# Buffers of their own for the turned queries and rows of maxima of one chunk of a linear attention and gated feed-forward kernel

## Chip, cores and metric

The program runs on one core of a Trainium2 chip. The metric is the device time of one execution in microseconds (us). Runs of the kernel before the change are given as the median of three.

## What is computed

Linear attention over 8 sequences of 576 tokens with 8 heads of 64, then a gated feed-forward over all 4608 tokens:

```python
q_s = exp(q - max(q, axis=-1)); q_s = q_s / (sum(q_s, axis=-1) + 1e-9)   # over a head's 64 entries
k_s = exp(k - max(k, axis=2));  k_s = k_s / (sum(k_s, axis=2) + 1e-9)    # over the tokens
kv  = einsum('bhsd,bhse->bhde', k_s, v)
x   = einsum('bhsd,bhde->bhse', q_s, kv)          # laid out as 4608 tokens x 512
out = ((x @ w_a) * (x @ w_b)) @ w_out             # 512 -> 1536 -> 512, all float32
```

## The kernel before

**Tiling.** The tokens are cut into 9 chunks of 512 (`c` = 0 to 8). The heads go in 4 pairs (`g` = 0 to 3), each with 128 features on the 128 partitions. For a chunk, attention gives `xf` (features by tokens), and the feed-forward takes it as its right-hand operand. Chunk 0 is done while the weights are converted from 64-bit words; from chunk 1 on the main loop runs over `c`, and inside it over 6 blocks `i` of 256 hidden features.

**Feed-forward.** Each block does seven products in the manner of Strassen and Winograd (`product`, L449, into the PSUM tiles `kx`, `ky`, `ka`, `kp`). A product is 12 matmuls of 128x256: two gates, two halves of the contraction, and three terms of a float32 number split in a high and a low part. The weights of each product (`ws`, 512 KB, 8 buffers) come from DRAM every time (`get_w`, L165). VectorE (DVE) and ScalarE (ACT) join the products in `cc` (L698 to L727) and split the gated result in `gh` and `gl`; `project` (L470) multiplies by `w_out` into `po`.

**Attention of the next chunk.** While chunk `c` is in the feed-forward, the attention of chunk `c + 1` is put between its instructions. `attention_tasks` returns a list of steps, and `Spread` hands out one of them at each of three calls per block (`attend`). What a step gives to DVE is queued behind the DVE instruction passed to the call (`issue_after`); loads, ScalarE and TensorE work have no such tie. From chunk 2 on (`LATE` = 2) a query is read twice: in token order (`qt`), for the maxima and the sums (`q_stats`), and turned (`qtt`, features by tokens), for the product. `q_stats_out` turns the statistics of all four pairs on TensorE (`pst`) and writes them to DRAM (`dq`). From there every head's row of negative maxima and row of reciprocal sums is read back, copied to 64 partitions (`mr`). `q_exp` adds the maxima (L354), takes the exponential (L355) and splits the result in `qh` and `ql` (L79, L82); `x_product` multiplies (`px`, L381), and L562 multiplies by the reciprocal sums into `xf`. These are the steps b0 (loads), b1 (`q_exp`) and b2 (product), in a pipeline over `g`: b0 of one pair stands in the step of b1 of the pair before it.

**Buffers.** `qtt` shares the two buffers of tag `kt` with the keys of the batch that the same chunk needs. `mr` has two buffers, `qh` and `ql` one each. Tag `wy` (8 buffers of 128x512) holds weights while they are converted and the sums of weight blocks that chunk 1 needs, and lies idle after that.

**Order.** A scheduler sets the order of each engine's instructions at build time, with a timeline of its own; at run time every engine works through its list in that order. All loads and stores of data are issued by SyncE (SP), in one list. A load waits there until its buffer is free, and everything behind it waits too. The loads use eight completion semaphores in turn, so a load also waits until the one eight places before it has landed.

Of the kernel before, what the change touches and what calls it, by code (L numbers as in the profile page):

```python
# [7 lines left out]
F32 = mybir.dt.float32  # L8
F32R = mybir.dt.float32r
# [4 lines left out]
ALU = mybir.AluOpType  # L14
# [15 lines left out]
def linear_attention_then_gated_ffn(  # L30
# [18 lines left out]
    nc = tc.nc  # L49
    B, NP, P, J, _, D = k.shape  # L50
# [4 lines left out]
    T = 512  # L55
# [20 lines left out]
    def split(hi, lo, src, hi_engine="act"):  # L76

        if hi_engine == "act":
            nc.scalar.copy(out=hi, in_=src)  # L79
        else:  # L80
            nc.vector.tensor_copy(out=hi, in_=src)
        nc.vector.tensor_tensor(out=lo, in0=src, in1=hi.bitcast(F32), op=ALU.subtract)  # L82
# [151 lines left out]
    def kv_soft_t(kt, tags):  # L234

        kf = kt.rearrange("p j c -> p (j c)")
        mc = sb.tile([P, 1], F32, name="mc")
        nc.vector.tensor_reduce(out=mc, in_=kf, axis=AX.X, op=ALU.max, negate=True)
        nc.scalar.activation(out=kf, in_=kf, func=AF.Exp, bias=mc)
        pa = ps.tile([P, J - 1, P], F32, name="pka", tag=tags[0])  # L240
        pb = ps.tile([P, P], F32, name="pkb", tag=tags[1])
        for j in range(J):
            nc.tensor.transpose(pa[:, j] if j < J - 1 else pb, kt[:, j], ident)
        nc.scalar.copy(out=kt[:, 0:J - 1], in_=pa)
        nc.vector.tensor_copy(out=kt[:, J - 1], in_=pb)
        return kt.rearrange("p j (h d) -> p j h d", h=2)

    def kv_product(kt, vt, tag="at"):
        pk = ps.tile([P, 2, D + 1], F32, name="pk", tag=tag)
        for j in range(J):  # L250
            nc.tensor.matmul(  # L251
                pk, kt[:, j].rearrange("p h d -> p (h d)"), vt[:, j],
                start=(j == 0), stop=(j == J - 1),
            )
        den = sb.tile([P, 1], F32, name="den")
        nc.vector.tensor_scalar_add(den, pk[:, 0, D:D + 1], EPS)
        nc.vector.reciprocal(out=den, in_=den)
# [83 lines left out]
    def q_turned(c, g, dq):  # L341

        qt = sb.tile([P, T], F32, name="qtt", tag="kt")
        nc.sync.dma_start(out=qt, in_=qt_late[c - LATE, g])
        mr = sb.tile([P, 2, T], F32, name="mr", bufs=2)
        for h in range(2):
            nc.sync.dma_start(
                out=mr[h * D:(h + 1) * D].rearrange("d w t -> d (w t)"),
                in_=dq[g, h].unsqueeze(0).broadcast_to([D, 2 * T]),
            )  # L350
        return qt, mr

    def q_exp(qt, mr):
        nc.vector.tensor_tensor(out=qt, in0=qt, in1=mr[:, 0], op=ALU.add)  # L354
        nc.scalar.activation(out=qt, in_=qt, func=AF.Exp)  # L355
# [132 lines left out]
    xfs = {}  # L488

    def attention_tasks(c):  # L490

        xfs[c] = sb.tile([P, NP, T], F32, name="xf", bufs=1)
        steps = []
        for b in range(c * T // S, (c * T + T - 1) // S + 1):
            if b in batch_done:
                continue
            batch_done.add(b)
            for g in range(NP):
                box = {}
# [12 lines left out]
        def pipeline(steps):  # L512

            parts = max((len(p) for p in steps), default=0)
            return [
                [steps[i - j][j] for j in range(parts) if 0 <= i - j < len(steps)]
                for i in range(len(steps) + parts - 1)
            ]

        if c < LATE:  # L520
            for g in range(NP):
                box = {}

# [12 lines left out]
        stats, last = [], []  # L536
        every = {}
        for g in range(NP):
            box = {}

            def a0(g=g, box=box):
                if g == 0:
                    every["st"] = sb.tile([P, NP, 2, 2, TT], F32, name="st", bufs=1)
                box["q"] = q_load(c, g)

            def a1(g=g, box=box):
                q_stats(box["q"], every["st"][:, g])
                if g == NP - 1:
# [5 lines left out]
            def b0(g=g, box=box):  # L554
                box["q"] = q_turned(c, g, every["dq"])

            def b1(box=box):
                box["e"] = q_exp(*box["q"])

            def b2(g=g, box=box):  # L560
                px = x_product(c, g, box["e"])
                nc.vector.tensor_tensor(out=xfs[c][:, g], in0=px, in1=box["q"][1][:, 1], op=ALU.mult)  # L562

            last.append((b0, b1, b2))
# [46 lines left out]
    for g in range(NP):  # L611
        kt, vt, qt = first[g]
        odd = g % 2
        kt = kv_soft_t(kt, (("at", "k0"), ("k1", "k2"))[odd])
# [5 lines left out]
        qhl = q_transpose(qt, ("at", "k1")[odd])  # L620
        px = x_product(0, g, qhl, ("po2", "po3")[odd])
# [43 lines left out]
    last = None  # L665
    for c in range(1, NCH):
# [4 lines left out]
        for i in range(NI):  # L671
# [29 lines left out]
            last = nc.vector.tensor_tensor(out=u3, in0=ka, in1=u2, op=ALU.add)  # L701
# [13 lines left out]
            last = nc.vector.tensor_tensor(out=cc[:, 3, 0], in0=cc[:, 3, 0], in1=cc[:, 3, 1], op=ALU.mult)  # L715
# [11 lines left out]
            last = nc.vector.tensor_tensor(out=cc[:, 2, 0], in0=cc[:, 2, 0], in1=cc[:, 2, 1], op=ALU.mult)  # L727
# [55 lines left out]
```

## Time and profile before

| | |
|---|---|
| runs | 988.35, 990.72, 991.26 us (median 990.72) |
| profiled execution | 984.57 us, of which the span from first to last instruction is 982.6 |
| mean granted TensorE clock | 0.991 |
| TensorE matmuls (PE) | busy 948.5 us, 6171 of them |
| weight loads of TensorE (PEld) | busy 851.9 us |
| VectorE (DVE) | busy 629.2 us |
| ScalarE (ACT) | busy 391.4 us |
| GpSimd (POOL) | busy 112.8 us |
| data queue of SyncE | 282.57 MB, 82.3% of the 16 DMA engines' time |

The feed-forward of chunk 2 starts at about 269.5 us of the span, that of chunk 3 at 371.3, of chunk 4 at 475.4, of chunk 5 at 576.8, of chunk 6 at 678.6, of chunk 7 at 780.6, of chunk 8 at 878.9. In the period of chunk `c` stands the attention of chunk `c + 1`. How to read it: "idle before <-releaser" is time in which an engine waited, and what ended the wait; idle time of an engine that nobody waits for costs nothing. A row of waits gives total time, number and the longest.

### The profile page before, as it was taken

Reading aid. Unit: us, or ns where it says so; the run is one execution under the profiler, and the core shown is the slowest. Engines: PE = TensorE matmul, PEld = TensorE weight load, DVE = VectorE, ACT = ScalarE, POOL = GpSimd, SP = SyncE. Lnnn points to the kernel's source line nnn. Section 1 sums busy time; section 2 is a strip of 40 time slices with the busy share of each in tenths; the row PEclk is TensorE's granted clock in tenths of the full one; section 3 lists DMA queues with packets and bytes.
Section 4 is the critical chain, followed back from the end, with each engine's and each line's share of the span. In section 5 each row is a group of like instructions: output and inputs, shape, how many; then the busy total and the mean of one; then the engine's idle time right before and its main releaser. Section 6 shows DMA issues by size and latency. Waiting matters only on the chain.

```text
span 982.6 us, 16989 instructions
## 1 busy us (share of the span) xinstructions
PE 948.5 (97%) x6171; PEld 851.9 (87%) x6171; DVE 629.2 (64%) x1257; ACT 391.4 (40%) x1085; POOL 112.8 (11%) x96
## 2 busy tenths in 40 slices
PE   4889999999999999999999999999999999999998
PEld 3657666899999999989999999999999999899997
DVE  7797786887685656656576557655666546653433
ACT  8665675632273325322442235223532263221101
POOL 3245345441000000000000000000000000000000
PEclk9799999999999999999999999999999999999999
DMA  9699858999989968997799779977998689767761
GB/s 347 222 412 402 343 207 294 373 327 305 301 285 352 320 237 280 325 328 250 248 335 324 271 251 345 319 270 257 331 299 299 220 300 283 274 224 271 246 207 61
DMA packets 93682, 283.64 MB, mean 289 GB/s; under 512 B 10848, under 2 KB 11424, under 8 KB 93600
## 3 DMA queue, kind: packets, MB, share of 16 engines
q1 hardware_dynamic: 93600, 282.57, 82.3%
q8 instruction: 49, 0.80, 0.3%
q14 instruction: 33, 0.27, 0.1%
HBM read 241.40 MB, written 37.98 MB: 284 GB/s over the span
## 4 chain that ended last, share of the span: by engine, by line
PE 78%; DMA 8%; DVE 5%; issue 4%; POOL 2%; ACT 2%; SPq 0%; POOLq 0%; DVEq 0%; ACTq 0%
PE po L470 25%; PE kp L449 13%; PE kx L449 13%; PE ka L449 12%; PE ky L449 6%; PE pk L251 3%; PE px L381 2%; POOL wr L103 2%; DMA mr<-dq 2%; PE po L459 2%; PE pt L426 2%; DMA qtt<-in_q_late 1%; DMA wo_raw<-in_w_out 1%; DMA dw<-ws 1%; DVE ws L82 1%
## 5 line engine op out<-in xcount | busy, mean ns | idle before, releaser
L470 PE MATMUL po<-wo_w,gh 128*128 128x512 f32 x768 | 227.2, 394 | 0.0
L449 PE MATMUL kx<-xo,ws 128*128 128x256 f32 x1152 | 164.5, 284 | 0.0
L449 PE MATMUL ka<-xo,ws 128*128 128x256 f32 x1152 | 162.3, 284 | 0.2
L470 PEld LDWEIGHTS po<-wo_w,gh 128*128 128x128 f32 x768 | 138.9, 189 | 26.2 <-ACT gh L79 0.3
L449 PE MATMUL kp<-xo,ws 128*128 128x256 f32 x1152 | 158.3, 284 | 0.8 <-DVE cc L712 0.8
L449 PEld LDWEIGHTS ka<-xo,ws 128*128 128x128 f32 x1152 | 151.2, 191 | 4.0 <-ACT xo L79 0.3
L449 PEld LDWEIGHTS kx<-xo,ws 128*128 128x128 f32 x1152 | 151.6, 191 | 3.4 <-issue 0.5
L449 PEld LDWEIGHTS kp<-xo,ws 128*128 128x128 f32 x1152 | 148.2, 191 | 3.6 <-DVE cc L712 1.0
L470 PE MATMUL po<-wo_w,gl 128*128 128x512 f32 x384 | 137.7, 396 | 0.0
L79 ACT CAST gh<-cc 128x512 fp32r<-128x512 f32 x96 | 57.7, 620 | 148.5 <-DVE cc L723 145.1
L722 DVE TENSOR_TENSOR cc<-kp,u 128x512 f32<-128x512 f32 x48 | 33.0, 688 | 89.2 <-PE kp L449 89.0
L323 ACT ACTIVATE qt<-qt,st 128x64 f32<-128x64 f32 x224 | 75.0, 337 | 31.7 <-DVE st L320 27.8
L470 PEld LDWEIGHTS po<-wo_w,gl 128*128 128x128 f32 x384 | 71.2, 188 | 15.8 <-DVE gl L82 0.4
L449 PE MATMUL ky<-xo,ws 128*128 128x256 f32 x576 | 79.4, 287 | 2.5 <-ACT xo L79 2.1
L426 PE MATMUL pt<-xo,ws 128*128 128x512 f32 x288 | 74.1, 406 | 4.0 <-ACT ga L433 3.2
L449 PEld LDWEIGHTS ky<-xo,ws 128*128 128x128 f32 x576 | 73.8, 194 | 3.2 <-ACT xo L79 2.4
L82 DVE TENSOR_TENSOR gl<-cc,gh 128x512 fp32r<-128x512 f32 x96 | 66.8, 703 | 9.4 <-ACT gh L79 9.2
L426 PEld LDWEIGHTS pt<-xo,ws 128*128 128x128 f32 x288 | 53.3, 188 | 20.4 <-ACT ga L433 4.7
L713 ACT COPY cc<-kx 128x256 f32<-128x256 f32 x48 | 17.8, 371 | 128.3 <-PE kx L449 120.6
L219 POOL PARTITION_ALL_REDUCE mx<-m x20 | 14.1, 704 | 470.9 <-DVE m L205 438.1
L712 DVE TENSOR_TENSOR cc<-kp,u 128x512 f32<-128x512 f32 x48 | 32.9, 684 | 52.3 <-PE kp L449 52.2
L355 ACT ACTIVATE qtt<-qtt 128x512 f32<-128x512 f32 x28 | 17.7, 633 | 107.4 <-DVE qtt L354 81.5
(126 smaller groups left out, 1238.7 us busy)
## 6 DMA issues: line engine op xcount, KB each, us to landing
ws<-dw SPq DMA_DIRECT2D x312, 512.0 KB, 5.3
dw<-ws SPq DMA_DIRECT2D x42, 512.0 KB, 4.9
mr<-dq SPq DMA_DIRECT2D x56, 256.0 KB, 6.3
raw<-in_w_ab SPq DMA_DIRECT2D x24, 512.0 KB, 8.1
out<-ot SPq DMA_DIRECT2D x36, 256.0 KB, 4.5
vt<-in_v SPq DMA_DIRECT2D x28, 325.0 KB, 7.5
qt<-in_q SPq DMA_DIRECT2D x32, 256.0 KB, 5.3
kt<-in_k SPq DMA_DIRECT2D x24, 320.0 KB, 6.0
```

The source lines that it names most:

```text
L79: nc.scalar.copy(out=hi, in_=src)
L82: nc.vector.tensor_tensor(out=lo, in0=src, in1=hi.bitcast(F32), op=ALU.subtract)
L103: nc.gpsimd.tensor_tensor(out=r, in0=u, in1=r, op=ALU.add)
L251: nc.tensor.matmul(pk, kt[:, j].rearrange("p h d -> p (h d)"), vt[:, j], start=(j == 0), stop=(j == J - 1),)
L323: nc.scalar.activation(out=qt[:, j, h], in_=qt[:, j, h], func=AF.Exp, bias=st[:, h, 0, j:j + 1], accum_out=st[:, h, 1, j:j + 1],)
L381: nc.tensor.matmul(px[:, s], w, m[:, s], start=(i == 0), stop=(i == 2))
L426: nc.tensor.matmul(pt, w[:, wp], x[g][:, xp], start=(i == 0), stop=(i == 3 * NP - 1))
L449: ins = nc.tensor.matmul(pt[:, n], w[:, n, wp, c], x[:, xp, c], start=(first and n == 0 and i == 0), stop=(i == 5), skip_group_check=True,)
L459: nc.tensor.matmul(po[t], g[:, t * P:(t + 1) * P], wo[f][:, 1].bitcast(F32), start=(f == 0), stop=(f == NF - 1),)
L470: ins = nc.tensor.matmul(po[t], a[:, ts], wo[f][:, w], start=(f == 0 and i == 0), stop=(f == NF - 1 and i == 2),)
L712: nc.vector.tensor_tensor(out=cc[:, 3], in0=kp, in1=u3, op=ALU.add)
L722: nc.vector.tensor_tensor(out=cc[:, 1], in0=kp, in1=u2, op=ALU.add)
```

## The change

For chunks 3 to 8 (`roomy`), the turned queries of pairs 0 and 1 go to the buffers of tags `qh` and `ql`, those of pairs 2 and 3 to `kt`. The rows of all four pairs go to the eight buffers of tag `wy`, maxima and reciprocal sums in separate tiles. The two parts of the split query, `qh` and `ql`, become one tile in tag `mr` and thereby have two buffers. The load step b0 leaves the pipeline: two steps of loads (pairs 0 and 1, then 2 and 3) stand ahead of it, so the list of steps grows from 12 to 13 (chunk 8: from 11 to 12). Every row of maxima and every row of sums is now loaded by a DMA of its own (64 partitions x 512) where one DMA (64 x 1024) brought both, also for chunk 2, whose order is otherwise as before in the source.

```diff
-        return dq.rearrange("(g h wj) p -> g h (wj p)", g=NP, h=2)
+        return dq.rearrange("(g h w j) p -> g h w (j p)", g=NP, h=2, w=2)
+    def roomy(c):
+        return c > LATE
+    def q_turned(c, g):
+        if roomy(c):
+            tag, bufs = (("qh", 1), ("ql", 1), ("kt", None), ("kt", None))[g]
+        else:
+            tag, bufs = "kt", None
+        qt = sb.tile([P, T], F32, name="qtt", tag=tag, bufs=bufs)
         nc.sync.dma_start(out=qt, in_=qt_late[c - LATE, g])
-        mr = sb.tile([P, 2, T], F32, name="mr", bufs=2)
+        return qt
+    def q_rows(c, g, dq):
+        if roomy(c):
+            rows = [sb.tile([P, T], F32, name=f"mr{w}", tag="wy", bufs=8) for w in range(2)]
+        else:
+            mr = sb.tile([P, 2, T], F32, name="mr", bufs=2)
+            rows = [mr[:, w] for w in range(2)]
         for h in range(2):
-            nc.sync.dma_start(
-                out=mr[h * D:(h + 1) * D].rearrange("d w t -> d (w t)"),
-                in_=dq[g, h].unsqueeze(0).broadcast_to([D, 2 * T]),
-            )
+            for w in range(2):
+                nc.sync.dma_start(
+                    out=rows[w][h * D:(h + 1) * D], in_=dq[g, h, w].unsqueeze(0).broadcast_to([D, T])
+                )
...
-        qh = sb.tile([P, T], F32R, name="qh", bufs=1)
-        ql = sb.tile([P, T], F32R, name="ql", bufs=1)
+        if roomy(c):
+            hl = sb.tile([P, 2, T], F32R, name="qhl", tag="mr", bufs=2)
+            qh, ql = hl[:, 0], hl[:, 1]
+        else:
+            qh = sb.tile([P, T], F32R, name="qh", bufs=1)
+            ql = sb.tile([P, T], F32R, name="ql", bufs=1)
...
+            last.append((b1, b2) if roomy(c) else (lambda t0=t0, r0=r0: (t0(), r0()), b1, b2))
...
+        if roomy(c):
+            seq += [rows[:2] + turned[:2], rows[2:] + turned[2:]]
         return seq + pipeline(last)
```

The first place is SP's list in the period of chunk 3, after the statistics of chunk 4 are written (`dq`). `ws` are weights, `vt` and `kt` values and keys of the next batch. Before:

```order
L338 DMA dq_4389<-sst 64x128
L165 DMA ws<-dw_681 128x1024
L165 DMA ws<-dw_774 128x1024
L347 DMA mr<-dq_4389 64x1024
L344 DMA qtt<-in_q_late 128x512
L347 DMA mr<-dq_4389 64x1024 x3
L165 DMA ws<-dw_2305 128x1024
L165 DMA ws<-dw_2324 128x1024
L165 DMA ws<-dw_2374 128x1024
L195 DMA vt<-in_v 128x650
L344 DMA qtt<-in_q_late 128x512
```

The same place in the list of the changed kernel, from the last three of the rows of `mr` on (13 more of them stand right ahead, behind the same `dq` and the weights 681 and 774):

```order
L364 DMA mr_4617<-dq_4405 64x512
L364 DMA mr_4616<-dq_4405 64x512
L364 DMA mr_4617<-dq_4405 64x512
L352 DMA qtt<-in_q_late 128x512 x2
L165 DMA ws<-dw_2311 128x1024
L165 DMA ws<-dw_2330 128x1024
L165 DMA ws<-dw_2382 128x1024
L165 DMA ws<-dw_788 128x1024
L165 DMA ws<-dw_2443 128x1024
L195 DMA vt<-in_v 128x650 x2
L165 DMA ws<-dw_893 128x1024
L352 DMA qtt<-in_q_late 128x512
```

Between the weights 774 and the next weights (2305 before, 2311 now, the same block) stood 5 loads, and now 18 stand there: 16 rows and the turned queries of pairs 2 and 3. The last `qtt` shown is pair 0 of the chunk after, a whole period ahead.

The second place is DVE's list in the third block of the same period. Before, the maxima of pair 0 are added (L354) ahead of the block's `cc`, and those of pair 1 behind three of its instructions:

```order
L354 TENSOR_TENSOR qtt<-qtt,mr 128x512
L256 TENSOR_SCALAR den<-pk 128x1
L257 RECIPROCAL den<-den 128x1
L259 SCALAR_TENSOR_TENSOR kv<-pk,den,mask 128x128
L81 CAST kvh_4471<-kv 128x128
L82 TENSOR_TENSOR kvl_4472<-kv,kvh_4471 128x128
L82 TENSOR_TENSOR ql<-qtt,qh 128x512
L712 TENSOR_TENSOR cc<-kp,u_4520 128x512
L715 TENSOR_TENSOR cc<-cc 128x256
L714 TENSOR_TENSOR cc<-kx,cc 128x256
L354 TENSOR_TENSOR qtt<-qtt,mr 128x512
```

In the changed kernel the addition for pair 0 is L370 and stands behind two instructions of `cc` of that block:

```order
L740 TENSOR_TENSOR cc<-kp,u_4536 128x512
L743 TENSOR_TENSOR cc<-cc 128x256
L370 TENSOR_TENSOR qtt<-qtt,mr_4537 128x512
L742 TENSOR_TENSOR cc<-kx,cc 128x256
L82 TENSOR_TENSOR qhl<-qtt,qhl 128x512
L750 TENSOR_TENSOR cc<-kp,u_4535 128x512
L751 TENSOR_TENSOR cc<-cc 128x256
L754 TENSOR_TENSOR cc<-ka,u_4535 128x512
L755 TENSOR_TENSOR cc<-cc 128x256
L370 TENSOR_TENSOR qtt<-qtt,mr_4543 128x512
```

Pair 0 moved to where pair 1 stood, one `attend` call later, and the other pairs follow in the same way.

More of the change, by code (lines that the diff above doesn't have):

```diff
@@ L338, in q_stats_out, with q_exp @@
         nc.sync.dma_start(out=dq, in_=sst)
-        return dq.rearrange("(g h wj) p -> g h (wj p)", g=NP, h=2)
-    def q_turned(c, g, dq):
-        qt = sb.tile([P, T], F32, name="qtt", tag="kt")
-        nc.sync.dma_start(out=qt, in_=qt_late[c - LATE, g])
-        mr = sb.tile([P, 2, T], F32, name="mr", bufs=2)
-        for h in range(2):
-            nc.sync.dma_start(
-                out=mr[h * D:(h + 1) * D].rearrange("d w t -> d (w t)"),
-                in_=dq[g, h].unsqueeze(0).broadcast_to([D, 2 * T]),
-            )
[L351 to L355, printed above, removed]
-        qh = sb.tile([P, T], F32R, name="qh", bufs=1)
-        ql = sb.tile([P, T], F32R, name="ql", bufs=1)
+        return dq.rearrange("(g h w j) p -> g h w (j p)", g=NP, h=2, w=2)
[7 more added lines that the diff above has]
+        qt = sb.tile([P, T], F32, name="qtt", tag=tag, bufs=bufs)
+        nc.sync.dma_start(out=qt, in_=qt_late[c - LATE, g])
+        return qt
[5 more added lines that the diff above has]
+            rows = [mr[:, w] for w in range(2)]
+        for h in range(2):
+            for w in range(2):
+                nc.sync.dma_start(
+                    out=rows[w][h * D:(h + 1) * D], in_=dq[g, h, w].unsqueeze(0).broadcast_to([D, T])
+                )
+        return rows
+    def q_exp(c, qt, rows):
+        nc.vector.tensor_tensor(out=qt, in0=qt, in1=rows[0], op=ALU.add)
+        nc.scalar.activation(out=qt, in_=qt, func=AF.Exp)
+        if roomy(c):
[4 more added lines that the diff above has]
+            ql = sb.tile([P, T], F32R, name="ql", bufs=1)
         split(qh, ql, qt)
@@ L535, in attention_tasks @@
             return pipeline(steps)
-        stats, last = [], []
+        stats, last, turned, rows = [], [], [], []
         every = {}
@@ L552, in attention_tasks, with t0, r0 @@
             box = {}
-            def b0(g=g, box=box):
-                box["q"] = q_turned(c, g, every["dq"])
+            def t0(g=g, box=box):
+                box["q"] = q_turned(c, g)
+            def r0(g=g, box=box):
+                box["r"] = q_rows(c, g, every["dq"])
             def b1(box=box):
-                box["e"] = q_exp(*box["q"])
+                box["e"] = q_exp(c, box["q"], box["r"])
             def b2(g=g, box=box):
                 px = x_product(c, g, box["e"])
-                nc.vector.tensor_tensor(out=xfs[c][:, g], in0=px, in1=box["q"][1][:, 1], op=ALU.mult)
-            last.append((b0, b1, b2))
+                nc.vector.tensor_tensor(out=xfs[c][:, g], in0=px, in1=box["r"][1], op=ALU.mult)
+            turned.append(t0)
+            rows.append(r0)
+            last.append((b1, b2) if roomy(c) else (lambda t0=t0, r0=r0: (t0(), r0()), b1, b2))
         stats, steps = pipeline(stats), pipeline(steps)
```

## The prediction

> **What bounds the kernel.** I read the page first, then stretches of one chunk period each, then the waits of TensorE between 262 and 880 us (where the changed attention steps lie), and last the timeline around those waits. The page and the table of stretches:
>
> ```profile
> PE 948.5 (97%) x6171; PEld 851.9 (87%) x6171; DVE 629.2 (64%) x1257; ACT 391.4 (40%) x1085; POOL 112.8 (11%) x96
> ```
> ```profile
> core 0: us, PE busy (x) PEld busy (x) DVE busy (x) ACT busy (x) POOL busy (x), PEclk, DMA share, GB/s
> ...
> 371.30:475.40 104.10, 102.54 (x716) 95.28 (x715) 64.09 (x139) 36.47 (x111) 2.81 (x4) 1.00 0.85 289
> 475.40:576.80 101.40, 101.40 (x716) 95.15 (x714) 63.01 (x139) 36.71 (x111) 2.81 (x4) 1.00 0.86 296
> 576.80:678.60 101.80, 101.80 (x716) 95.55 (x715) 64.22 (x139) 37.02 (x111) 2.81 (x4) 1.00 0.86 295
> 678.60:780.60 102.00, 102.00 (x716) 95.59 (x714) 64.22 (x139) 36.70 (x111) 2.81 (x4) 1.00 0.84 287
> 780.60:878.90 98.30, 97.07 (x663) 89.91 (x662) 53.65 (x103) 33.58 (x107) 0.00 (x0) 1.00 0.79 268
> ```
>
> TensorE is the bound: in three of these periods it never rests, at full clock, and 716 matmuls take 101.4 to 102.0 us. No other engine is near its limit. So the change can win only where TensorE waits, and that is little:
>
> ```profile
> PE px L381 <- DVE ql L82: 1.8, 3, 1.2
> PE kp L449 <- DVE cc L712: 0.8, 1, 0.8
> PE px L381 <- ACT qh L79: 0.3, 1, 0.3
> ```
>
> 2.9 us in all between 262 and 880 us. DVE, in the same stretch, waits far longer for the loads that the change moves:
>
> ```profile
> DVE qtt L354 <- DMA mr<-dq: 31.8, 15, 4.5
> DVE qtt L354 <- DMA qtt<-in_q_late: 12.6, 4, 3.4
> ```
>
> 44.4 us, of which nearly all is hidden behind TensorE's queue of work. The third chunk's period shows where it is not. DVE's timeline there:
>
> ```profile
> 413.91 0.69 DVE L354 TENSOR_TENSOR qtt<-qtt,mr 128x512 f32<-128x512 f32 x1 [2.64 <-DMA mr<-dq]
> 421.33 0.69 DVE L354 TENSOR_TENSOR qtt<-qtt,mr 128x512 f32<-128x512 f32 x1 [3.14 <-DMA qtt<-in_q_late]
> 430.75 0.69 DVE L354 TENSOR_TENSOR qtt<-qtt,mr 128x512 f32<-128x512 f32 x1 [3.18 <-issue]
> 439.17 0.69 DVE L354 TENSOR_TENSOR qtt<-qtt,mr 128x512 f32<-128x512 f32 x1 [4.12 <-DMA kt<-in_k]
> 440.38 0.68 DVE L712 TENSOR_TENSOR cc<-kp,u 128x512 f32<-128x512 f32 x1
> ```
>
> Four additions of maxima wait 13.1 us for loads, and the `cc` queued behind the last one comes late. TensorE pays there, and once more near 840 us:
>
> ```profile
> 434.50 0.39 PE L381 MATMUL px<-ql,kvh 128*128 128x256 f32 x1 [0.34 <-DVE ql L82]
> 438.94 1.35 PE L449 MATMUL ka<-xo,ws 128*128 128x256 f32 x10
> 441.11 0.51 PE L449 MATMUL kp<-xo,ws 128*128 128x256 f32 x2 [0.82 <-DVE cc L712]
> 442.38 0.38 PE L381 MATMUL px<-ql,kvh 128*128 128x256 f32 x1 [0.29 <-DVE ql L82]
> 839.05 0.40 PE L449 MATMUL kx<-xo,ws 128*128 128x256 f32 x2
> 840.66 0.50 PE L381 MATMUL px<-ql,kvh 128*128 128x512 f32 x1 [1.22 <-DVE ql L82]
> ```
>
> **What the waits are worth.** Idle time understates it, since a matmul counts as busy beyond the start of the next one. The third chunk took 104.1 us for the 716 matmuls that the fourth did in 101.4, so its waits cost 2.7 us where the table shows 1.56 idle. Near 840 us the two `kx` start 0.12 apart (price below), the next matmul could have started at 839.29 and did at 840.66: 1.4 us. The 0.3 us on `qh` costs about 0.3. Together 4.4 us is the most that the six periods can give back; 2.9 us (idle alone) is the low value. I take 4.4, since the period of 104.1 us is a measured length and not a modelled end. The Trainium skill says this too (Perfetto Trace Analysis, Identifying the Most-Contended Engine): busy time of matmuls is a bad measure of the room left because they are pipelined. The 104.1 against 101.4 us agrees.
>
> **The change part by part.**
>
> *The loads that DVE waited for.* SP held them back because a row of `mr` waited for the product before it, and a turned query for a buffer of `kt`; in these six periods:
>
> ```profile
> SPq L347 <- DVE xf L562: 28.9, 10, 4.1
> SPq L344 <- DVE ql L82: 18.1, 10, 4.1
> SPq L165 <- PE kp L449: 106.1, 36, 5.6
> ```
>
> With eight tiles for rows the first wait goes. The turned queries of pairs 0 and 1 are issued a period ahead, those of pairs 2 and 3 once the keys are used. So when DVE comes to an addition, its operands have landed. I take the 4.4 us as won, less 0.2 for a `px` that still meets a late `ql`: the lists put such products close behind the split.
>
> Is anything late next? I followed TensorE's new list through the third period by pitches (0.12 us for a 256-wide matmul, 1.44 for twelve):
>
> ```profile
> 419.94 0.28 PE L381 MATMUL px<-qh,kvh 128*128 128x256 f32 x1
> 425.69 1.60 PE L449 MATMUL ky<-xo,ws 128*128 128x256 f32 x12
> 427.13 1.60 PE L449 MATMUL ka<-xo,ws 128*128 128x256 f32 x12
> ```
>
> ```profile
> 417.34 0.42 DVE L715 TENSOR_TENSOR cc<-cc 128x256 f32<-128x256 f32 x1
> ```
> ```profile
> L355 ACT ACTIVATE qtt<-qtt 128x512 f32<-128x512 f32 x28 | 17.7, 633 | 107.4 <-DVE qtt L354 81.5
> ```
> The product of pair 0 now follows two more products, at 419.94 + 24 x 0.12 = 422.8. Its `ql` needs DVE's addition behind `cc` (from 417.8, 0.69 us), then the exponential (0.63) and a copy of about the same length on ScalarE, and a subtraction of 0.69 on DVE: 420.5, so 2.3 us in hand. Pairs 1 to 3 have 2.4 us or more by the same count. The step added (13 for 15 calls) ends in the fifth block of six, a block ahead of the next chunk's first operands, so it costs nothing; without that cover it would be one call, some 5 us a period.
>
> *Arithmetic.* The number, form and engine of DVE, ScalarE and TensorE instructions do not change; 0. The split query's second buffer only removes a wait. The tiles of tag `wy` are free by then: GpSimd, the last to use them, has only its four maxima of keys a period left (2.81 us x4).
>
> *Sixteen DMAs of half the size for eight.* 56 more over the run. Bytes are the same. What counts is SP's list, where 18 loads now stand in a row ahead of the weights (5 before). The old issues there, and the times to landing of weights, rows and the small `dq`:
>
> ```profile
> 406.27 0.45 SPq L347 DMA_DIRECT2D mr<-dq  x1
> 406.90 0.46 SPq L344 DMA_DIRECT2D qtt<-in_q_late  x1
> 407.40 1.73 SPq L347 DMA_DIRECT2D mr<-dq  x3
> 409.18 1.73 SPq L165 DMA_DIRECT2D ws<-dw  x3
> ```
> ```profile
> ws<-dw SPq DMA_DIRECT2D x312, 512.0 KB, 5.3
> mr<-dq SPq DMA_DIRECT2D x56, 256.0 KB, 6.3
> dq<-sst SPq DMA_DIRECT2D x7, 32.0 KB, 2.9
> ```
>
> A row costs SP 1.73/3 = 0.58 us, so 16 rows 9.3 and two queries 0.9: the weights go out at 406.3 + 10.2 = 416.5 instead of 409.2. They are the ones for `ky` at 425.69, or 424.9 by the new order, in which the product of pair 1 (six matmuls of 0.12) has moved behind it. With 5.3 us to land they are there at 421.8: 3.1 us in hand. The next weights follow at 0.4 us each for products 1.44 us or more apart, so the first is the tight one. This term is 0 by that count. From below it cannot gain. From above: with eight loads in flight, each landing after the median 6.3 us, 18 loads take 18/8 x 6.3 = 14.2 us, and weights that then need the slow landing of that stretch,
>
> ```profile
> DMA to landing us min/median/max: 3.6/8.1/9.2
> ```
>
> arrive at 406.3 + 14.2 + 8.1 = 428.6, that is 3.7 us late, up to 22 us in six periods. I take 0, since halves are nearer to the 32 KB row (2.9 us) than to a landing of 6.3 that was measured behind 512 KB of weights. The same halves in the period of chunk 1 (8 of them in a row for 4) stand where four of seven weights are made on chip, and cost 0. Elsewhere SP's extra 56 x 0.58 = 32 us is covered by its waits for free weight buffers (106.1 us for `kp` alone).
>
> The Trainium skill speaks against this edit (DMA: Bandwidth & Descriptors, Rules for kernel authors): small transfers should be coalesced, and two transfers to disjoint halves of the partitions only serialize. The kernel already paid the halves; the change doubles their number. By the rule the burst costs as in the first rival, and the sum is 997 instead of 986.5.
>
> **Sum.** -4.4 + 0.2 + 0 = -4.2 us. Against the profiled execution 984.57 gives 980.4. The median of the runs shown is 6.2 us above that execution, and nothing here tells where those lie, so I carry the difference over: 990.72 - 4.2 = 986.5 (-0.42%).
>
> **Rivals.**
>
> *The burst starves TensorE of weights (slower).* Place: the first `ky` weights behind the 18 loads, every period. It decides once burst plus landing exceeds 424.9 - 406.3 = 18.6 us, against 15.5 by my count and 22.3 by the upper one. Halfway to the upper end, 1.8 us in each of six periods, 11 us less the 4.2 won: 997. For it: landings of 8.1 us in that very stretch. Against: half the bytes in flight.
>
> *The waits were hidden anyway.* DVE's loads come early, but TensorE still meets late `ql`, because the additions are tied behind `cc` one call later than before and margins are only 2 us. Then 1 to 2 us are won: 989.2, no change that can be measured.
>
> *More is won.* The 6.2 us of the unprofiled runs are also waits for such loads, and half of them go: 986.5 - 3.1 = 983.4. Nothing in the profile speaks for it beyond the size of DVE's waits.
>
> **Chances.** Operands early and nothing late next: 0.55; the waits stay hidden: 0.22; the burst starves: 0.17; more is won: 0.06. About 0.3% (3 us) is what a measurement of this kernel tells from none. The first case has a spread of some 1.5 us around -4.2 and so is faster in four of five: 0.45, with 0.10 the same. With the fourth, faster 0.50. The burst case is the same in a quarter of its outcomes (a short lateness that eats the gain): same 0.36, slower 0.14. The range, 984 to 994, takes in the second case and the burst with up to 1.3 us a period (990.7 - 4.2 + 7.5), and leaves out the worst bursts and the larger gains, some 2 in 10.
>
> **What the new profile would show.** Right: DVE's 44 us of waits for `mr` and `qtt` fall below 10, the third chunk's period comes to 101.5 us, and the 1.2 us wait near 840 goes. The burst takes about 10 us of SP and weights still land some 3 us ahead of their product. Wrong, if TensorE's weight loads wait for the DMA of `ws`, if periods 2 to 6 grow together by the same amount, or if `px` still waits for `ql` in several periods.

## The result and the profile after

The changed kernel takes 981.82 us (median of 6 executions, 980.89 to 985.94), the kernel before 988.48 us beside it (median of 6, 987.0 to 991.26). The ratio is 0.9932, with a 95% interval of 0.9915 to 0.9949: 6.7 us faster. That is a larger gain than forecast (4.2 us, to 986.5), and the time lies below the range (984 to 994). The profiled execution of the changed kernel took 982.17 us (span 980.2, clock 0.991), only 2.4 us less than the one of before that the prediction was read from (984.57). So the two profiled executions differ by a third of what the medians differ by. That gap is the question of the experiments. A part of the miss is the baseline and no matter of the change: the forecast of 986.5 started from 990.72, the median of three executions, and the median of six is 988.48, 2.2 us lower.

The page of the changed kernel, its engines:

```profile
PE 946.8 (97%) x6171; PEld 851.7 (87%) x6171; DVE 632.7 (65%) x1257; ACT 392.9 (40%) x1085; POOL 113.3 (12%) x96
```

Its table of stretches, cut within 0.2 us of the start of the feed-forward of chunks 2 to 8:

```profile
270.00:373.60 103.60, 102.59 (x720) 95.88 (x719) 70.00 (x149) 41.13 (x119) 3.29 (x4) 1.00 0.84 299
373.60:474.80 101.20, 101.20 (x716) 94.96 (x715) 63.92 (x139) 37.08 (x111) 2.81 (x4) 1.00 0.84 297
474.80:576.10 101.30, 101.30 (x715) 95.06 (x714) 63.86 (x138) 36.89 (x111) 2.81 (x4) 1.00 0.84 297
576.10:677.80 101.70, 101.70 (x715) 95.47 (x715) 64.06 (x138) 36.89 (x111) 2.81 (x4) 1.00 0.85 296
677.80:779.90 102.10, 102.10 (x716) 95.69 (x715) 64.21 (x139) 36.96 (x111) 2.81 (x4) 1.00 0.83 287
779.90:876.40 96.50, 96.50 (x663) 89.75 (x662) 54.15 (x103) 34.02 (x107) 0.00 (x0) 1.00 0.78 268
sum 606.40, PE 605.39 PEld 566.80 DVE 380.20 ACT 222.96 POOL 14.53; mean PE 100.90 PEld 94.47 DVE 63.37 ACT 37.16 POOL 2.42
```

From chunk 3 on TensorE never rests. The period of chunk 3 went from 104.1 to 101.2 us, that of chunk 7 (which holds the wait near 840 us) from 98.3 to 96.5. From the first matmul of chunk 2 to that of chunk 8 the six periods take 606.6 us (269.9 to 876.5); in the first trace of before they took 878.9 - 269.5 = 609.4. The two hold not quite the same work. In the changed kernel, six matmuls of the last product of chunk 2's own attention fall behind the start of chunk 2. From chunk 3 to chunk 7 both run the same number of matmuls (3513 in each trace), and there the time went from 507.6 us (371.3 to 878.9) to 502.8 (373.7 to 876.5): 4.8 us less, while chunk 3 starts 2.4 us later.

All waits of TensorE and, of DVE's waits, the one for the moved loads, between 262 and 880 us:

```profile
PE px L401 <- ACT qh L79: 0.9, 1, 0.9
...
DVE qtt L370 <- DMA mr<-dq: 5.8, 3, 3.8
```

TensorE's 2.9 us became 0.9; DVE's 44.4 us became 5.8, and the wait for a turned query is gone. The 0.9 us and 3.8 of the 5.8 belong to the last pair of chunk 2, whose rows still go to the two buffers of `mr`, now by twice as many loads. Before (SP and DVE):

```profile
256.03 1.09 SPq L347 DMA_DIRECT2D mr<-dq  x2
264.79 0.69 DVE L354 TENSOR_TENSOR qtt<-qtt,mr 128x512 f32<-128x512 f32 x1 [2.50 <-DMA mr<-dq]
```

After (SP, DVE and TensorE):

```profile
258.76 3.24 SPq L364 DMA_DIRECT2D mr<-dq  x4
269.09 0.69 DVE L370 TENSOR_TENSOR qtt<-qtt,mr 128x512 f32<-128x512 f32 x1 [3.85 <-DMA mr<-dq]
271.14 0.33 PE L401 MATMUL px<-qh,kvh 128*128 128x128 f32 x1 [0.88 <-ACT qh L79]
```

The addition comes 4.3 us later, and this product of chunk 2 with it. DVE's timeline in the third period shows the four additions that waited 13.1 us before:

```profile
419.35 0.69 DVE L370 TENSOR_TENSOR qtt<-qtt,mr 128x512 f32<-128x512 f32 x1
...
426.44 0.69 DVE L370 TENSOR_TENSOR qtt<-qtt,mr 128x512 f32<-128x512 f32 x1
...
430.99 0.68 DVE L370 TENSOR_TENSOR qtt<-qtt,mr 128x512 f32<-128x512 f32 x1
...
438.03 0.68 DVE L370 TENSOR_TENSOR qtt<-qtt,mr 128x512 f32<-128x512 f32 x1
```

No row has a bracket: none of them waits. The price stands in SP's timeline, here in the third and in the fourth period:

```profile
405.66 0.47 SPq L338 DMA_DIRECT2D dq<-sst  x1
407.02 0.85 SPq L165 DMA_DIRECT2D ws<-dw  x2
409.19 10.18 SPq L364 DMA_DIRECT2D mr<-dq  x16
419.48 0.99 SPq L352 DMA_DIRECT2D qtt<-in_q_late  x2
420.52 3.08 SPq L165 DMA_DIRECT2D ws<-dw  x5
...
509.04 12.11 SPq L364 DMA_DIRECT2D mr<-dq  x16
```

The list of DMAs gives the size and median landing of these loads:

```profile
ws<-dw SPq DMA_DIRECT2D x312, 512.0 KB, 5.3
...
mr<-dq SPq DMA_DIRECT2D x112, 128.0 KB, 4.3
```

How near the burst comes to hurting is seen on the first weights behind it. They are issued at 420.52, the landing of that single load is below, and the product that needs them follows in TensorE's timeline:

```profile
DMA to landing us min/median/max: 5.2/5.2/5.2
```
```profile
427.30 1.60 PE L469 MATMUL ky<-xo,ws 128*128 128x256 f32 x12
```

420.52 + 5.2 = 425.7, which is 1.6 us ahead of 427.30. Worked out in the same way for every load of weights, the least lead in the periods of chunks 2 to 7 is 2.1, 1.6, 0.7, 2.3, 1.0 and 1.9 us. In the kernel before it was 6.6 to 7.6 us. The cover is nearly used up, but it holds.

### The profile page after: what moved, and what is told of

It reads as the page before. It is cut to its first block, busy times and chain, and to the rows that moved or that the text cites. A ratio compares the mean times of both kernels' runs of the same rounds, so it can differ in the third digit from the quotient of the medians.

```text
span 980.2 us, 17037 instructions
## 1 busy us (share of the span) xinstructions
PE 946.8 (97%) x6171; PEld 851.7 (87%) x6171; DVE 632.7 (65%) x1257; ACT 392.9 (40%) x1085; POOL 113.3 (12%) x96
## 4 chain that ended last, share of the span: by engine, by line
PE 73%; DVE 2%; DMA 2%; SPq 1%; ACT 1%; issue 1%; DVEq 0%
PE po L490 25%; PE ka L469 12%; PE kp L469 12%; PE kx L469 12%; PE ky L469 6%; PE pk L251 2%; PE px L401 2%; DMA mr<-dq 1%; DMA dw<-ws 1%; DVE ws L82 1%; SPq L364 1%; ACT qt L323 0%; DVE gl L82 0%; DVE m L203 0%; DVE m L204 0%
## 5 line engine op out<-in xcount | busy, mean ns | idle before, releaser
L490 PE MATMUL po<-wo_w,gh 128*128 128x512 f32 x768 | 229.7, 395 | 0.1
L490 PE MATMUL po<-wo_w,gl 128*128 128x512 f32 x384 | 139.9, 396 | 0.0
L726 ACT COPY u<-kx 128x512 f32<-128x512 f32 x48 | 28.0, 583 | 81.2 <-PE kx L469 81.0
```

The costliest lines, as they stand in the source:

```text
L490: ins = nc.tensor.matmul(po[t], a[:, ts], wo[f][:, w], start=(f == 0 and i == 0), stop=(f == NF - 1 and i == 2),)
L726: nc.scalar.copy(out=u2, in_=kx)
```

## The experiments

There are eleven runs on three chips; each ratio is to the kernel before, run beside it on the same chip. The table puts the profiled execution of each beside its time. "Rows" is DVE's wait in L354 (or the line it became) for `mr` between 262 and 880 us, "TensorE" the sum of its listed waits there, "six periods" the time from the start of the feed-forward of chunk 2 to that of chunk 8, read from the timeline (start and end in brackets), and "chunks 3 to 7" the last five of them alone. In these five all kernels run the same matmuls, but for one product (12 matmuls) more in spread and one less in mixed and spread.

| kernel | median us (executions) | ratio, 95% interval | rows | TensorE | six periods | chunks 3 to 7 |
|---|---|---|---|---|---|---|
| before, first trace | 988.48 (6) | 1 | 31.8 | 2.9 | 609.4 (269.5 to 878.9) | 507.6 |
| before again | 989.57 (12) | 0.9994, 0.9969 to 1.0019 | 42.5 | 6.3 | 613.2 (269.4 to 882.6) | 509.5 |
| halved rows only | 990.92 (12) | 1.0006, 0.9986 to 1.0027 | 46.9 | 5.1 | 614.7 (271.2 to 885.9) | 510.6 |
| turned queries only | 990.61 (12) | 0.9992, 0.9971 to 1.0014 | 40.7 | 2.2 | 609.9 (270.3 to 880.2) | 507.5 |
| before, 7 weight buffers | 994.42 (12) | 1.0027, 0.9999 to 1.0055 | 44.3 | 7.3 | 612.1 (271.8 to 883.9) | 509.1 |
| mixed and spread | 991.55 (12) | 1.0007, 0.9982 to 1.0032 | 44.1 | 7.0 | 615.3 (269.9 to 885.2) | 510.9 |
| changed | 981.82 (6) | 0.9932, 0.9915 to 0.9949 | 5.8 | 0.9 | 606.6 (269.9 to 876.5) | 502.8 |
| changed again | 982.18 (6) | 0.9926, 0.9900 to 0.9953 | 5.9 | 0.5 | 606.2 (271.4 to 877.6) | 502.8 |
| rows and second split buffer | 983.14 (9) | 0.9939, 0.9916 to 0.9961 | 5.4 | 1.6 | 607.8 (269.7 to 877.5) | 503.9 |
| rows only | 984.80 (6) | 0.9943, 0.9922 to 0.9964 | 7.2 | 2.5 | 609.3 (269.3 to 878.6) | 504.1 |
| mixed | 981.68 (6) | 0.9907, 0.9879 to 0.9936 | 8.2 | 1.4 | 607.3 (270.9 to 878.2) | 503.0 |
| spread | 981.73 (6) | 0.9905, 0.9877 to 0.9934 | 14.7 | 0.4 | 605.7 (270.4 to 876.1) | 504.9 |
| changed, 7 weight buffers | 986.21 (12) | 0.9946, 0.9924 to 0.9969 | 3.6 | 6.1 | 612.7 (274.2 to 886.9) | 508.2 |

The last column parts the two kinds: with 8 weight buffers it is 502.8 to 504.9 us where the rows come early and 507.5 to 510.9 where they come late.

### Before, once more

The kernel before, unaltered, with a second profile.

> The kernel before, unchanged, to see another execution's trace. The profiled execution of before took 984.57 us, the median of its runs 988.5; the changed kernel gained 6.7 us by the medians but 2.4 us by the two profiled executions. Theory L (late additions): an ordinary execution of before loses more at the same places, the additions of maxima that wait for rows and turned queries. Then this trace, if it takes some 988 us, shows 6 to 8 us lost by TensorE between 262 and 880 us (the old trace: 4.4), at waits for ql, qh and cc, and the stretch before 262 us is as long as in the old trace. Theory E (elsewhere): the extra 4 us lie ahead of 262 us or in a lower clock, and the six periods lose 4 to 5 us as before. Ratio to before 1.000 by both, within 0.3%.

Measured: 989.57 us (984.17 to 996.67), profiled execution 988.29 us, span 986.3. Its waits of TensorE between 262 and 880 us:

```profile
PE px L381 <- DVE ql L82: 3.1, 3, 2.0
PE px L381 <- ACT qh L79: 1.7, 3, 0.9
PE kp L449 <- DVE u L699: 0.9, 1, 0.9
PE kp L449 <- DVE cc L712: 0.6, 1, 0.6
```

and the sum row of its table of stretches over the same six periods:

```profile
sum 613.20, PE 606.98 PEld 566.95 DVE 376.75 ACT 219.70 POOL 14.08; mean PE 101.16 PEld 94.49 DVE 62.79 ACT 36.62 POOL 2.35
```

The span is 3.7 us longer than in the first trace, and the six periods alone are 3.8 us longer (613.2 for 609.4). The stretch ahead of them (269.4 for 269.5 us) and the last chunk (103.7 us in both) are equal. So what this execution, near the median, loses over the first profiled one lies where the additions of maxima stand: 1.8 us in the period of chunk 2 and 1.9 in those of chunks 3 to 7. Near 842 us, the place of the 1.22 us wait of the first trace, TensorE's and DVE's timelines now show:

```profile
844.33 0.50 PE L381 MATMUL px<-ql,kvh 128*128 128x512 f32 x1 [1.96 <-DVE ql L82]
```
```profile
841.78 0.69 DVE L354 TENSOR_TENSOR qtt<-qtt,mr 128x512 f32<-128x512 f32 x1 [4.09 <-DMA mr<-dq]
```

The row of maxima came later, and the same chain (row, addition, `ql`, `px`) cost 0.7 us more. Against this execution the changed kernel's periods of chunks 3 to 7 are 6.7 us shorter (509.5 - 502.8). It reaches chunk 3 only 0.6 us later (373.7 for 373.1), and its span is 6.1 us shorter.

### The rows alone

The changed kernel without its early turned queries and without the second buffer of the split query: rows go to the eight tiles of `wy` in one step.

```diff
-            tag, bufs = (("qh", 1), ("ql", 1), ("kt", None), ("kt", None))[g]
+            tag, bufs = "kt", None
...
-            hl = sb.tile([P, 2, T], F32R, name="qhl", tag="mr", bufs=2)
+            qh = sb.tile([P, T], F32R, name="qh", bufs=1)
+            ql = sb.tile([P, T], F32R, name="ql", bufs=1)
...
-            seq += [rows[:2] + turned[:2], rows[2:] + turned[2:]]
+            seq[-1] = seq[-1] + rows
```

> Rows of maxima and sums of all four pairs at once in their eight tiles, for chunks 3 to 8; the turned queries stay in the two buffers of kt and in the pipeline of steps, and the split query keeps single buffers. Theory L with rows as the main cause (31.8 us of DVE's waits were for mr, and mr waited 28.9 us in SP's queue): most of the gain, ratio 0.994 to 0.996. If the turned queries, each waiting for a buffer of kt, decide as much, half: 0.996 to 0.998. If only both together free SP's queue: 0.999 to 1.001. Wait of DVE for mr under 8 us, for qtt still over 10.

Measured: 984.80 us, ratio 0.9943 (0.9922 to 0.9964). DVE's waits at the addition:

```profile
DVE qtt L367 <- DMA qtt<-in_q_late: 23.6, 10, 4.4
DVE qtt L367 <- DMA mr<-dq: 7.2, 3, 3.9
```

The rows are the effective part: the wait for `mr` fell to 7.2 us and most of the gain is there, although DVE waits longer than before for the turned queries (23.6 us for 12.6) and the split query has its single buffers.

### The turned queries alone

The reverse: early turned queries and more buffers for the split query (in `wy`), rows as before, in the two buffers of `mr`.

```diff
-            rows = [sb.tile([P, T], F32, name=f"mr{w}", tag="wy", bufs=8) for w in range(2)]
+        mr = sb.tile([P, 2, T], F32, name="mr", bufs=2)
...
-            hl = sb.tile([P, 2, T], F32R, name="qhl", tag="mr", bufs=2)
+            qh = sb.tile([P, T], F32R, name="qhx", tag="wy", bufs=8)
+            ql = sb.tile([P, T], F32R, name="qlx", tag="wy", bufs=8)
...
-            seq += [rows[:2] + turned[:2], rows[2:] + turned[2:]]
+            seq[-1] = seq[-1] + turned
```

> Turned queries of chunks 3 to 8 early, in the buffers of qh, ql and kt; the split query goes to two tiles of the idle weights' tag; the rows stay as before, one DMA a head in the two buffers of mr and in the pipeline. If rows are the main cause: ratio 0.997 to 1.000, and DVE still waits some 30 us for mr. If the turned queries decide: 0.994 to 0.996. If both are needed: 0.999 to 1.001.

Measured: 990.61 us, ratio 0.9992 (0.9971 to 1.0014): nothing. DVE no longer waits for `qtt<-in_q_late`, but the additions are as late as ever:

```profile
DVE qtt L366 <- DMA mr<-dq: 40.7, 18, 4.9
```

An addition needs both operands, and the row is the one that comes last.

### Halved rows in the kernel before

Only the DMAs are changed: every row by one of its own, into the same two buffers, at the same place.

```diff
...
-            nc.sync.dma_start(
-                out=mr[h * D:(h + 1) * D].rearrange("d w t -> d (w t)"),
-                in_=dq[g, h].unsqueeze(0).broadcast_to([D, 2 * T]),
-            )
+            for w in range(2):
+                nc.sync.dma_start(
+                    out=mr[h * D:(h + 1) * D, w], in_=dq[g, h, w].unsqueeze(0).broadcast_to([D, T])
+                )
```

> The kernel before, with every row loaded by a DMA of its own (64 partitions x 512) instead of one for both rows of a head: the doubled number of DMAs alone, 56 more. My count: hidden, ratio 0.999 to 1.002; a row costs SP about 0.6 us, so each pair's rows go out 1.2 us later and DVE waits some 1 us more for each, 28 us in all, mostly covered. If the halves are dear where rows are already late: 1.002 to 1.006.

Measured: 990.92 us, ratio 1.0006 (0.9986 to 1.0027). Twice the number of DMAs for the same bytes costs nothing that the medians tell from none; the interval leaves room for 2.7 us. One wait of TensorE looks like a wait for weights:

```profile
PE px L381 <- DMA ws<-dw: 1.8, 1, 1.8
```

It is a late row again. The weights of the product behind it had landed long before (the least lead of weights in this run is 3.9 us). On DVE, ScalarE and TensorE the chain is the addition, the cast to `qh` that ends at 446.27, and the product that reads it:

```profile
444.27 0.69 DVE L354 TENSOR_TENSOR qtt<-qtt,mr 128x512 f32<-128x512 f32 x1 [5.59 <-DMA mr<-dq]
445.65 0.62 ACT L79 CAST qh<-qtt 128x512 fp32r<-128x512 f32 x1
446.32 0.39 PE L381 MATMUL px<-qh,kvh 128*128 128x256 f32 x1 [1.81 <-DMA ws<-dw]
```

A price of the halves does show in one place of the traces, the attention of chunk 2, where every variant with halved rows still uses the two buffers of `mr`. Its last addition starts at 264.4 to 264.8 us in the three executions with whole rows and 8 weight buffers, and at 266.9 to 270.7 in the eight with halves. Chunk 3 starts at 371.3 to 373.1 in those three, and at 373.6 to 375.3 in the others (spread, 371.2, has one product less ahead of it).

### A smaller burst, and a burst spread out

Two variants of the changed kernel that take away part of its burst. In the first ("mixed"), rows of pairs 0 and 1 go to `mr` with one DMA a head, so that 14 loads stand in a row instead of 18:

```diff
...
-        if roomy(c):
+        if roomy(c) and g > 1:
...
+        elif roomy(c):
+            mr = sb.tile([P, 2, T], F32, name="mr", bufs=2)
+            for h in range(2):
+                nc.sync.dma_start(
+                    out=mr[h * D:(h + 1) * D].rearrange("d w t -> d (w t)"),
+                    in_=dq[g, h].rearrange("w t -> (w t)").unsqueeze(0).broadcast_to([D, 2 * T]),
+                )
+            return [mr[:, w] for w in range(2)]
...
```

(and the split query goes to `wy`). In the second ("spread"), every pair's rows are loaded in the step of its addition, on SP behind the weights that were ordered last:

```diff
...
+                with tc.issue_after(latest["ws"].ins):
+                    box["r"] = q_rows(c, g, every["dq"])
...
+            last.append((lambda r0=r0, b1=b1: (r0(), b1()), b2) if roomy(c) else (lambda t0=t0, r0=r0: (t0(), r0()), b1, b2))
...
```

> The changed kernel, with the rows of pairs 0 and 1 in the two tiles of mr, one DMA a head (64 x 1024), those of pairs 2 and 3 in four tiles of the idle weights' tag as halves, and the split query in the other four. 14 loads in a row ahead of the weights instead of 18; on SP about 4 x 0.6 + 8 x 0.63 + 1.0 = 8.4 us instead of 11.2. Theory S (the burst only uses up spare time): least lead of the weights 3 to 5 us instead of 0.7 to 2.3, time as the changed kernel, ratio to before 0.992 to 0.995. Theory B (the burst already costs TensorE waits in ordinary executions): 2 to 4 us faster than the changed kernel, 0.988 to 0.991.

> The changed kernel's buffers, but rows of a pair queued on SP behind the latest weights, so that the rows of pair 3 go out behind two more weights (12 rows and one or two queries, two weights, 4 rows), and the steps as early as before the change (12, not 13). Theory S: as the changed kernel, 0.992 to 0.995, least lead of the weights 2 to 4 us. If the later step matters (additions one call later than before), a little faster: 0.990 to 0.992.

Measured: 981.68 us (0.9907, 0.9879 to 0.9936) and 981.73 us (0.9905, 0.9877 to 0.9934). The least leads of the weights became 1.5 to 2.7 us and 1.1 to 3.7 us, for 0.7 to 2.3; 3 to 5 and 2 to 4 us were expected. The changed kernel did not run on that chip; against its ratios of 0.9932 and 0.9926 the intervals overlap. Both ratios lie where a gain over the changed kernel was expected to put them, but that a smaller burst wins anything is not shown.

### One weight buffer less

The changed kernel and the kernel before with 7 weight buffers instead of 8:

```diff
-        return sb.tile([P, 2, 2, 2, P], F32R, name="ws", bufs=8)
+        return sb.tile([P, 2, 2, 2, P], F32R, name="ws", bufs=7)
```

> The changed kernel with 7 buffers for weights instead of 8, which takes some 2.2 us (one product's turn) from the lead of every weight. The least lead in each of six periods was 0.7 to 2.3 us, so in each the first weights behind the 18 loads now land up to 1.5 us late: TensorE waits for the DMA of ws, 3 to 8 us in all, ratio to before 0.996 to 1.002. If leads are longer in ordinary executions: 0.993 to 0.996, like the changed kernel with 8.

> The kernel before with 7 buffers for weights, the control for the run on the changed kernel with 7. Least lead of weights before was 6.4 to 7.6 us, so 2.2 us less costs nothing in the six periods; a lost buffer may cost up to 2 us while weights are converted. Ratio 0.999 to 1.003.

Measured for the changed kernel: 986.21 us, 982.16 to 992.57 in 12 executions, where mixed and spread with 8 buffers took 980.09 to 983.86 on the same chip. The profiled one is the longest of the twelve, and TensorE waits 4.1 us for weights in it:

```profile
PE kx L469 <- DMA ws<-dw: 2.2, 2, 1.8
...
PE ka L469 <- DMA ws<-dw: 1.9, 1, 1.9
```

The kernel before with 7 buffers has no such wait (the least lead in each of the six periods is 3.9 to 6.2 us); its ratio of 1.0027 (0.9999 to 1.0055) leaves open whether it is slower at all. So the burst has a price, and it is hidden by the last weight buffer. The ratio of the changed kernel with 7 buffers, 0.9946 (0.9924 to 0.9969), is better than was expected for a burst that starves TensorE, and its interval overlaps that with 8; what shows the price is the wait.

### The changed kernel again, and two variants beside it

The changed kernel ran unaltered on another chip, with two variants. In the first, the turned queries are loaded as in the kernel before, and all else is as changed (the edit of "rows only" without its middle part). The second is mixed and spread at once.

> The changed kernel unaltered, beside before on one chip, as the yardstick of the two variants that run with it. Theory L (the loss of the additions of maxima that come late is larger in ordinary executions of before than in its first profiled one, and the change takes it away): again about 6.7 us faster than before, ratio 0.991 to 0.995, and a profiled execution of 981 to 984 us, near the median, since nothing is left that varies. Theory P (the first profiled pair, 984.57 and 982.17 us, told the true size, and the medians of 6.7 us apart were luck of the sample): 2 to 4 us, ratio 0.996 to 0.998.

> The changed kernel without its early turned queries: they are loaded as in before, a step ahead of their addition, into the two buffers of tag kt; rows in eight tiles at once, split query with two buffers. DVE should wait 20 us or more for qtt<-in_q_late, as in the variant with rows alone. If the early turned queries add something once the rows come early, this is 1 to 3 us slower than the changed kernel on the same chip (983 to 985 us for 982); if the rows (and the second buffer) are the whole of it, both agree within 1 us.

> Both variants of the burst together: rows of pairs 0 and 1 in the two buffers of mr by one DMA a head, rows of pairs 2 and 3 by halves in the tiles of tag wy, the split query in wy too, and each row's load behind the weights ordered last. If the burst of 18 loads still costs the changed kernel something that its 8 weight buffers do not hide, this is 1 to 2 us faster than the changed kernel on the same chip (ratio to before 0.990); if the cover is whole, the same within 1 us. The least lead of the weights should be above the changed kernel's 0.7 to 2.3 us in most periods.

The changed kernel: 982.18 us for 990.49, ratio 0.9926 (0.9900 to 0.9953), profiled 983.29. The gain stands, at 6.7 us or somewhat more (8.3 by these medians, 0.74% by the ratio); the 2 to 4 us of the first pair of profiles do not. Its least leads of weights are 0.6 to 2.4 us. The six periods in its table of stretches:

```profile
sum 606.20, PE 605.59 PEld 567.14 DVE 380.54 ACT 222.67 POOL 14.53; mean PE 100.93 PEld 94.52 DVE 63.42 ACT 37.11 POOL 2.42
```

Without the early turned queries: 983.14 us (0.9939, 0.9916 to 0.9961), 1.0 us more than the changed kernel, which such intervals do not tell from nothing. DVE's waits at the addition, of this variant:

```profile
DVE qtt L367 <- DMA qtt<-in_q_late: 22.0, 10, 4.2
DVE qtt L367 <- DMA mr<-dq: 5.4, 3, 2.0
```

So 22 us of waits for turned queries stay hidden almost wholly (1.1 us more in the periods of chunks 3 to 7), while the executions with 32 to 47 us of waits for rows take 4.7 to 8.1 us longer there than the changed kernel's 502.8.

Mixed and spread together missed what was expected by far: 991.55 us, ratio 1.0007 (0.9982 to 1.0032). The cover of the weights was as good as expected (the least lead is 3.7 us in the period of chunk 2, 5.7 to 7.7 in the others), but the whole gain is gone. DVE's waits and TensorE's largest wait say why:

```profile
DVE qtt L380 <- DMA mr<-dq: 44.1, 15, 5.3
```
```profile
PE px L411 <- ACT qhx L79: 3.8, 3, 2.4
```

The third period on SP, and on DVE:

```profile
410.32 0.45 SPq L364 DMA_DIRECT2D mr<-dq  x1
...
421.87 4.67 SPq L374 DMA_DIRECT2D mr<-dq  x4
426.83 0.34 SPq L354 DMA_DIRECT2D qtt<-in_q_late  x1
427.49 6.24 SPq L167 DMA_DIRECT2D ws<-dw  x5
433.78 2.67 SPq L374 DMA_DIRECT2D mr<-dq  x4
```
```profile
433.77 0.69 DVE L380 TENSOR_TENSOR qtt<-qtt,mr 128x512 f32<-128x512 f32 x1 [3.54 <-DMA mr<-dq]
...
445.26 0.69 DVE L380 TENSOR_TENSOR qtt<-qtt,mr 128x512 f32<-128x512 f32 x1 [5.34 <-DMA mr<-dq]
```

SP's largest wait in this stretch (426 to 437 us) is:

```profile
SPq L167 <- DMA ws<-dw: 4.1, 2, 2.3
```

The rows of pair 3 go out at 433.78, behind five weights whose issue takes 6.24 us, 4.1 of it waiting until earlier weights have landed. DVE's last addition starts at 445.26 instead of about 438. TensorE comes to that pair's product and waits:

```profile
447.32 0.58 PE L411 MATMUL px<-qhx,kvh 128*128 128x256 f32 x1 [2.35 <-ACT qhx L79]
```

The span is 991.0 us, 9.7 more than that of the changed kernel on the same chip. This is the plainest test of the cause, though it was not made for it: all buffers are there, only the rows are late again, and the time is that of the kernel before.

## Why the prediction was wrong, point by point

**The bound and the mechanism: right.** TensorE bounds both kernels, DVE's waits for the moved loads fell below 10 us (5.8), the third period came to 101.2 us (101.5 forecast), and the wait near 840 us is gone. In the table above every kernel whose rows come early is faster, and every kernel whose rows come late is not, whatever else was changed.

**The step that failed: "nothing here tells where those lie, so I carry the difference over".** The 4.4 us that the loads could give back were sized from one execution, and the 6.2 us between it and the median were taken for time that the change does not touch. The second trace of before loses 3.7 us more in the six periods and none elsewhere. In the periods of chunks 3 to 7, where the work is equal, that execution of before, near its median, takes 509.5 us and the changed kernel 502.8 in both its traces. The halved-rows kernel, whose execution of 991.52 is near its median too, takes 510.6. The term for an ordinary execution is therefore about 6.7 us instead of 4.4, and the median moved by 6.7. For the first execution alone the term was well sized: 507.6 - 502.8 = 4.8 us.

**A second term: the halves in the period of chunk 1, put at 0.** The prediction held that these loads cost nothing where they stand. In the traces the last addition of chunk 2 comes 4.3 us later in the changed kernel than in the first trace of before, and chunk 3 starts 2.4 us later. Against the second trace it is 0.6 us. So the first pair of profiles shows -4.8 + 2.4 = -2.4 us, and the second trace against the same changed kernel -6.7 + 0.6 = -6.1, which are the differences of the spans. How much of the 0.6 to 2.4 us the halves cost in an ordinary execution is not told by the medians.

**The rival that came nearest** was "more is won", with a chance of 0.06 and half of the 6.2 us (983.4). Its mechanism was right, and its 4.2 + 3.1 = 7.3 us is close to the 6.7 measured. That its time still lies 1.6 us above the measured one is luck of the sample: three executions gave it a baseline 2.2 us above that of six. The prediction held that nothing in the profile spoke for it beyond the size of DVE's waits. That size was the evidence: 44 us of waits for loads, of which the trace showed two places that were no longer hidden, are hidden for the most part in one execution and less in the next.

**Which loads matter: counted alike, and they are not.** The prediction added the waits for rows and for turned queries to one sum. The early turned queries alone win nothing (0.9992), the rows alone 0.9943. It did name the two reasons of SP's list separately (`xf` for `mr`, `ql` for `kt`), and only the first turned out to matter. Of the 13.1 us that it put down to loads in the third period, 3.18 carry `<-issue`, which names no load.

**The burst: hidden as forecast, but with less to spare.** Forecast were 9.3 us for 16 rows, 0.9 for two queries and 3.1 us in hand. Measured were 10.18 and 12.11 us for 16 rows in two periods, 0.99 us for two queries, and a least lead of 0.7 to 2.3 us. Part of the miss is the start: the burst began at 409.19 us in the third period, where the count began at 406.3. The landing of the halves (median 4.3 us) lay between the two rows that bounded it (2.9 and 6.3). With 7 weight buffers the first rival, starved weights, does occur: 4.1 us of waits in the profiled execution.

The halves alone measured 1.0006 (0.9986 to 1.0027). The Trainium skill (DMA: Bandwidth & Descriptors, Rules for kernel authors) advises to coalesce small transfers and holds two transfers to disjoint partition halves to be pointless, since they serialize. The case of 997 us that the prediction drew from it did not come: the medians leave room for at most 2.7 us. The traces agree with it in so far as four halves took SP 3.24 us where two whole rows took 1.09, at the one place where rows still wait for buffers.

**What stays open.** Why the rows land later in one execution of the kernel before than in another was not found; their median landing is 6.3 us in the first trace and 6.7 in the second. The second trace (988.29 us) is still 1.3 us short of its median, so the last microsecond is inferred from medians and not seen. Whole rows for chunk 2, with all else as changed, stand untested. Whether mixed or spread beats the changed kernel by less than 2 us is not told apart either.

## What to carry to other kernels

Before a gain is sized from waits, ask whether the profiled execution is an ordinary one: where its time lies below the median, the waits under suspicion are probably larger in the others, and two or three executions compared stretch by stretch say where. Compare such stretches where both kernels do the same work: a product that slips over the cut, as the one of chunk 2 did here, looks like a loss or a gain. Large waits of an engine off the critical path that are hidden with margins of a microsecond or two are a cost in waiting, so count them by their margin and not by what showed once. And a load that is issued early in the list only helps while what stands behind it still has buffers ahead: look at the least lead of the next operands, and keep urgent loads ahead of those that have to wait in the list.

## What was not expected

The executions of the kernel before spread widely (984.17 to 999.61 us in 41 on one chip), those of the changed kernel little (980.12 to 985.94 in 12 on two): in these samples the time without the waits for rows is narrower as well as shorter. Mixed and spread, with its rows late again, spreads over 986.89 to 995.03 in 12. And the two variants that each kept the gain lost it together: spread alone placed all its rows between 407 and 420 us of the third period, while with mixed the last rows came at 433.78, because five weights stood ahead of them that had to wait until earlier loads had landed.
